# Moving four groups of on-chip buffers by 64 to 352 bytes in an attention and feed-forward kernel

## The chip, the cores and the metric

The kernel runs on one core of one Trainium2 chip. A core has a matrix engine (TensorE, PE in the profile, with its weight loads shown apart as PEld), a vector engine (VectorE, DVE), a scalar engine (ScalarE, ACT), GpSimd (POOL), a queue engine (SyncE, SP) and 16 DMA engines. On-chip memory (SBUF) has 128 partitions; a tile has the same byte address in each of its partitions. The accumulators lie in a second memory, PSUM. The metric is the device time of one execution in microseconds. Before the change two runs took 795.97 and 796.78 us, median 796.38 us.

## The reference, cut to what matters

Attention within chunks of 64 tokens, for 8 batches of 8 heads with 576 tokens and 64 columns a head, and then a feed-forward layer on the 4608 tokens, with 512 model columns, 2048 hidden columns and a leaky rectifier with one slope for each hidden column:

```python
scores = scale * np.matmul(q_c, k_c.transpose(0, 1, 2, 4, 3))
scores = scores - np.max(scores, axis=-1, keepdims=True)
attn = np.exp(scores)
attn = attn / (np.sum(attn, axis=-1, keepdims=True) + 1e-09)
out = np.matmul(attn, v_c)
...
h = x @ w_in
g = np.maximum(h, 0.0) + alpha * np.minimum(h, 0.0)
return (g @ w_out).astype(np.float32)
```

## The kernel before, in words

Every wide product is made of three matmuls on numbers split into a rounded high part and the rest (`hi` and `lo`, type float32r): high by high, high by low, low by high. A wide matmul has 128 rows, 128 columns of weights and 512 moving columns, and each is preceded by its own load of weights.

The tokens are nine blocks of 512. Blocks 0 to 2 (`PLAIN`) are done directly: `first_layer` (L394) multiplies a weight tile `wi` by the tokens `xh` and `xl` into the PSUM tile `ps_h`; the rectifier makes the tile `g` and its split `gh`, `gl`; `ffn_out` (L430) takes 128-column slices of `gh` and `gl` as weights and the tile `wo` as the moving operand. While this runs, the weights are fetched into tiles named `raw`, `more`, `wi` and `wo` and split by DVE and ACT, the remaining attention is done a part at a time (`attn_scores` L246, `attn_softmax`, `attn_blocks`, `attn_values` L361), and sums and differences of weight quarters are written to DRAM.

Blocks 3 to 8 are done in three pairs by a seven-product scheme on 2 by 2 blocks: `first_product` (its matmuls are in `product`, L695), then `second_product` (L836). Their weights come back from DRAM through a ring of four buffers of 512 KB: `stream` (L636, issued from POOL's queue) fills in turn two buffers `raw` of the pool `stage` and the buffers `wi15` and `wo15` of the pool `const`. One buffer serves 12 matmuls, and a buffer is refilled when the matmuls that read it are done. The moving operands of L695 lie in `const`; those of L836 are made in turn in `gh` and `gl` (or `g`) of the pool `gp`, and in `ta`, `tb`, `more` (once `ob`) of `stage`.

Order and place: a list of tokens (`START`) and then the program's own order, with priorities for some parts, set the order on each engine. SBUF tiles come from pools that are laid out one after another in the order in which they are opened (L96 to L102): `small`, `const` (weights), `load` (q, k, v and the transposed softmax), `soft`, `xp` (x), `gp` (pieces of g), `stage` (staging tiles). Every tile from `const` on has a size that is a multiple of 512 bytes a partition, and `const` begins at byte 5120, so all of them begin at a multiple of 512.

Two of the small products matter for the argument. `attn_scores` takes as weights and as moving operand the same 64 columns of two tiles; `attn_values` takes columns h*64 on of `v_sb` as weights, and as moving operand two runs of 32 columns of `pT` that begin at (4*par+hp)*128 bytes (h = 2*hp + par):

```python
lhsT=q_sb[rows, 2 * hp + c],  rhs=kb[rows, 2 * hp + c],                       # L246
lhsT=v_sb[rows, h * C:(h + 1) * C],  rhs=p[rows, :, par * NP + hp],           # L361
```

Of the kernel before, what the change touches and what calls it, by code (L numbers as in the profile page):

```python
# [11 lines left out]
F32 = mybir.dt.float32  # L12
# [48 lines left out]
def tile_local_attention_prelu_ffn(  # L61
# [13 lines left out]
    P = 128  # L75
# [19 lines left out]

    small = ctx.enter_context(tc.tile_pool(name="small", bufs=1))  # L96
    const = ctx.enter_context(tc.tile_pool(name="const", bufs=1))
    load = ctx.enter_context(tc.tile_pool(name="load", bufs=1))
    soft = ctx.enter_context(tc.tile_pool(name="soft", bufs=1))
    xp = ctx.enter_context(tc.tile_pool(name="xp", bufs=2))  # L100
    gp = ctx.enter_context(tc.tile_pool(name="gp", bufs=2))
    stage = ctx.enter_context(tc.tile_pool(name="stage", bufs=2))  # L102
    dram = ctx.enter_context(tc.tile_pool(name="dram", bufs=1, space=bass.MemoryType.DRAM))
    ps_a = ctx.enter_context(tc.tile_pool(name="ps_a", bufs=1, space=bass.MemoryType.PSUM))
# [956 lines left out]
```

## Time and profile before

| | before |
|---|---|
| two runs, us | 795.97, 796.78 |
| the profiled execution, us | 797.23 |
| its span, first to last instruction, us | 795.5 |
| granted TensorE clock over the span | 1.000 |
| PE busy | 783.7 us (99%) |
| DVE busy | 650.7 us (82%) |
| ACT busy | 449.8 us (57%) |
| POOL busy | 205.9 us (26%) |
| DMA | 192.40 MB, mean 242 GB/s |

The profiled execution lasted 1.7 us longer than its span; that is time before the first and after the last instruction. Matmuls are pipelined: one lasts some 390 ns in the records while the next begins some 227 ns after it, so PE's busy time alone does not tell whether it could go faster; the distance between the starts does.

### The profile page before, as it was taken

What the parts mean: (1) busy time and instruction counts of PE and PEld (TensorE: products, weight loads), DVE (VectorE), ACT (ScalarE), POOL (GpSimd) and SP (SyncE); (2) the same over time, 40 slices, a digit from 0 to 9 for tenths busy, and PEclk for the clock granted to TensorE, in tenths of its full rate; (3) what the DMA queues carried; (4) which work ended last, traced back from release to release, by engine and by line L of the source; (5) the groups of instructions that cost most, each with busy time, mean ns of one, the idle gap of its engine ahead of it and who ended that gap; (6) DMA issues with size and microseconds to landing.
All of it is one profiled execution on the core that took longest, in us unless ns stands there. A gap on an engine that the chain in (4) does not pass through costs nothing.

```text
span 795.5 us, 15528 instructions
## 1 busy us (share of the span) xinstructions
PE 783.7 (99%) x5562; PEld 641.8 (81%) x5562; DVE 650.7 (82%) x1147; ACT 449.8 (57%) x1223; POOL 205.9 (26%) x326
## 2 busy tenths in 40 slices
PE   7999999999999999999999999999999999999998
PEld 6788888888878888888887788888887888888886
DVE  6999989997979976887799987777899856677875
ACT  6975545656667565656665636664565524354552
POOL 0053323442424420111112341111222421112232
PEclk9999999999999999999999999999999999999999
DMA  9769495566869675888767799876567985565788
GB/s 349 316 220 357 176 310 195 205 225 184 266 199 263 231 272 179 281 262 278 265 211 243 212 285 322 271 227 197 187 217 231 264 293 185 188 208 186 243 227 243
DMA packets 73404, 192.40 MB, mean 242 GB/s; under 512 B 11488, under 2 KB 18928, under 8 KB 73200
## 3 DMA queue, kind: packets, MB, share of 16 engines
q0 software_dynamic: 38272, 127.43, 50.4%
q1 hardware_dynamic: 34768, 63.60, 23.7%
q8 instruction: 44, 0.72, 0.4%
q10 hardware_dynamic: 288, 0.39, 0.2%
q14 instruction: 32, 0.26, 0.1%
HBM read 135.27 MB, written 42.99 MB: 224 GB/s over the span
## 4 chain that ended last, share of the span: by engine, by line
PE 91%; DVE 5%; ACT 3%; DMA 0%; issue 0%; SPq 0%; DVEq 0%; ACTq 0%
PE ps_o L695 29%; PE ps_o L836 16%; PE ps_h L394 16%; PE ps_b L836 8%; PE ps_ob L430 8%; PE ps_oa L430 8%; PE ps_a L361 2%; DVE wi L755 2%; PE ps_a L246 2%; DVE gl L655 1%; ACT wo L289 1%; ACT wi L289 1%; PE ps_h L897 1%; DMA k_sb<-kT 0%; DVE tb L655 0%; DVE more L655 0%
## 5 line engine op out<-in xcount | busy, mean ns | idle before, releaser
L394 PE MATMUL ps_h<-xh,wi 128*128 128x512 f32 x384 | 104.5, 393 | 0.2 <-ACT xh L346 0.2
L695 PE MATMUL ps_o<-wi,raw 128*128 128x512 f32 x252 | 99.1, 393 | 0.1
L695 PE MATMUL ps_o<-wo,raw 128*128 128x512 f32 x252 | 98.1, 389 | 0.0
L394 PEld LDWEIGHTS ps_h<-xh,wi 128*128 128x128 f32 x384 | 71.1, 188 | 15.3 <-ACT xh L346 0.4
L263 ACT ACTIVATE pr<-ps_a,mx 128x64 f32<-128x64 f32 x224 | 67.5, 328 | 0.9
L430 PE MATMUL ps_ob<-wo,gh 128*128 128x512 f32 x192 | 59.3, 390 | 1.1 <-ACT g L461 1.1
L430 PE MATMUL ps_oa<-wo,gh 128*128 128x512 f32 x192 | 59.9, 393 | 0.0
L695 PEld LDWEIGHTS ps_o<-wi,raw 128*128 128x128 f32 x252 | 47.3, 188 | 10.4 <-ACT wi L461 0.2
L695 PEld LDWEIGHTS ps_o<-wo,raw 128*128 128x128 f32 x252 | 47.3, 188 | 9.6
L394 PE MATMUL ps_h<-xl,wi 128*128 128x512 f32 x192 | 52.0, 390 | 0.0
L654 ACT CAST gh<-wi 128x512 fp32r<-128x512 f32 x45 | 28.1, 624 | 40.4 <-PE ps_o L836 29.4
L695 PE MATMUL ps_o<-wi,wo 128*128 128x512 f32 x126 | 49.6, 393 | 0.0
L695 PE MATMUL ps_o<-wi,wi 128*128 128x512 f32 x126 | 49.5, 393 | 0.0
L263 ACT ACTIVATION_READ_ACCUMULATOR pr<-ps_a,mx 128x1 f32 x224 | 49.2, 220 | 0.0
L695 PE MATMUL ps_o<-wo,wi 128*128 128x512 f32 x126 | 49.1, 389 | 0.0
L695 PE MATMUL ps_o<-wo,wo 128*128 128x512 f32 x126 | 49.1, 389 | 0.0
L408 ACT CAST gh<-g 128x512 fp32r<-128x512 f32 x48 | 30.2, 630 | 32.1 <-DVE g L382 24.8
L636 POOL DMA_DIRECT2D raw<-wi_a x42 | 22.4, 532 | 97.7 <-PE ps_o L695 86.2
L717 DVE TENSOR_TENSOR gh<-ps_o,gh 128x512 f32<-128x512 f32 x24 | 16.6, 691 | 37.3 <-ACT gh L716 21.0
L379 ACT ACTIVATE wo<-gh 128x512 f32<-128x512 f32 x24 | 15.2, 632 | 53.1 <-DVE gh L725 53.1
L636 POOL DMA_DIRECT2D raw<-wo_a x42 | 22.4, 532 | 85.5 <-PE ps_o L836 45.2
L430 PEld LDWEIGHTS ps_ob<-wo,gh 128*128 128x128 f32 x192 | 36.0, 188 | 9.0 <-ACT g L461 1.5
(295 smaller groups left out, 2138.8 us busy)
## 6 DMA issues: line engine op xcount, KB each, us to landing
raw<-wi_a POOLq DMA_DIRECT2D x42, 512.0 KB, 4.9
raw<-wo_a POOLq DMA_DIRECT2D x42, 512.0 KB, 4.3
wi<-wi_a POOLq DMA_DIRECT2D x21, 512.0 KB, 4.1
wo<-wi_a POOLq DMA_DIRECT2D x21, 512.0 KB, 4.2
wi<-wo_a POOLq DMA_DIRECT2D x21, 512.0 KB, 4.1
wo<-wo_a POOLq DMA_DIRECT2D x21, 512.0 KB, 4.4
k_sb<-kT SPq DMA_DIRECT2D x28, 256.0 KB, 4.7
q_sb<-qT SPq DMA_DIRECT2D x28, 256.0 KB, 3.8
```

The lines of the kernel that those rows point to most:

```text
L246: pe(nc.tensor.matmul(ps[c * C:(c + 1) * C, par, (NP + hp) * C:(NP + hp + 1) * C], lhsT=q_sb[rows, 2 * hp + c], rhs=kb[rows, 2 * hp + c], ...
L263: last = nc.scalar.activation(pr[:, g], sc3[:, g // NP, g % NP], AF.Exp, bias=mx[:, g], scale=SCALE, accum_out=sm[:, g])
L289: last = nc.scalar.activation(pr[:, g], sc3[:, g % 2, g // 2], AF.Exp, bias=mx[:, g], scale=SCALE, accum_out=sm[:, g])
L361: pe(nc.tensor.matmul(ps[par * C:(par + 1) * C, c, hp * C:(hp + 1) * C], lhsT=v_sb[rows, h * C:(h + 1) * C], rhs=p[rows, :, par * NP + hp] ...
L394: pe(nc.tensor.matmul(hps, lhsT=wi[f][:, l, k * P:(k + 1) * P], rhs=xx[:, k], start=(i == 0 and k == 0), stop=(i == 2 and k == NK - 1),))
L408: nc.scalar.copy(gh, g)
L430: pe(nc.tensor.matmul(o, lhsT=a[:, ts], rhs=wo[f][:, l], start=(f == first and i == 0), stop=(f == last and i == 2),))
L636: streamed[0] = nc.gpsimd.dma_start(out=f32(t), in_=units[side][n])
L654: hi = nc.scalar.copy(t_hi, t)
L695: pe(nc.tensor.matmul(ps, lhsT=w[:, l, k * P:(k + 1) * P], rhs=xx[:, xl], start=first and at == 0, stop=at == n - 1, skip_group_check=not ...
L717: nc.vector.tensor_tensor(t, d, t, op=ALU.add)
L836: pe(nc.tensor.matmul(ps[m], lhsT=w[:, l, m * P:(m + 1) * P], rhs=xx, start=i != 6 and j == 0 and n == 0, stop=j == JF - 1 and n == 2, ski ...
```

## The change

Four pools of one buffer each are opened in front of `load`, `xp`, `gp` and `stage`, and one small tile is made in each that nothing reads or writes. They take 64, 64, 128 and 96 bytes a partition.

```diff
     const = ctx.enter_context(tc.tile_pool(name="const", bufs=1))
+    shift_load = ctx.enter_context(tc.tile_pool(name="shift_load", bufs=1))
+    shift_load.tile([P, 16], F32, name="shift_load")
     load = ctx.enter_context(tc.tile_pool(name="load", bufs=1))
     soft = ctx.enter_context(tc.tile_pool(name="soft", bufs=1))
+    shift_xp = ctx.enter_context(tc.tile_pool(name="shift_xp", bufs=1))
+    shift_xp.tile([P, 16], F32, name="shift_xp")
     xp = ctx.enter_context(tc.tile_pool(name="xp", bufs=2))
+    shift_gp = ctx.enter_context(tc.tile_pool(name="shift_gp", bufs=1))
+    shift_gp.tile([P, 32], F32, name="shift_gp")
     gp = ctx.enter_context(tc.tile_pool(name="gp", bufs=2))
+    shift_stage = ctx.enter_context(tc.tile_pool(name="shift_stage", bufs=1))
+    shift_stage.tile([P, 24], F32, name="shift_stage")
     stage = ctx.enter_context(tc.tile_pool(name="stage", bufs=2))
```

The first byte of some tiles in the two built programs, and what is left modulo 512:

```
pool (tile)         before            after
const (wi15, wo15)  9216, 5120    0   9216, 5120      0
load (q_sb)         136192        0   136256         64
soft (pr)           152576        0   152640         64
xp (xh)             154624        0   154752        128
gp (g)              187392        0   187648        256
stage (raw)         199680        0   200032        352
stage (ob, the end) 228352            228704
```

The two programs have the same instructions in the same order on each of PE, DVE, ACT, POOL and SP, with the same tiles and the same waits; only the line numbers behind L97 are 2 to 8 higher.

## Rows read from the trace of the kernel before

**Rows 1.** The page: the span, the busy time of the engines, and the shares of the chain of work that ended last.

```profile
span 795.5 us, 15528 instructions
PE 783.7 (99%) x5562; PEld 641.8 (81%) x5562; DVE 650.7 (82%) x1147; ACT 449.8 (57%) x1223; POOL 205.9 (26%) x326
...
PE 91%; DVE 5%; ACT 3%; DMA 0%; issue 0%; SPq 0%; DVEq 0%; ACTq 0%
```

**Rows 2.** The same chain in order of time, some of its pieces: start in us, length in us, what, how many instructions.

```profile
45.08 2.72 PE ps_h L394 x12
47.80 1.36 PE ps_oa L430 x6
...
639.31 76.16 PE ps_o L695 x336
...
726.35 32.64 PE ps_o L836 x144
```

**Rows 3.** PE's instructions in order of time around one visit of the attention, at 322 us: start, length from the first start to the last end, line, count.

```profile
322.00 0.39 PE L695 MATMUL ps_o<-wi,wo 128*128 128x512 f32 x1
322.22 0.39 PE L695 MATMUL ps_o<-wo,wo 128*128 128x512 f32 x1
322.54 0.69 PE L361 MATMUL ps_a<-pT,v_sb 64*64 64x64 f32 x32
323.06 0.65 PE L246 MATMUL ps_a<-k_sb,q_sb 64*64 64x64 f32 x32
```

**Rows 4.** All instructions of L361, and of L246, of the whole span: count, and minimum, median and maximum of one in ns.

```profile
L361 PEld LDWEIGHTS ps_a<-pT,v_sb x896: 128/135/136, 163.7 to 551.8; 64*64 64x64 f32 x180
L361 PE MATMUL ps_a<-pT,v_sb x896: 217/218/268, 163.7 to 551.8; 64*64 64x64 f32 x180
...
L246 PEld LDWEIGHTS ps_a<-k_sb,q_sb x896: 129/135/136, 140.2 to 531.0; 64*64 64x64 f32 x180
L246 PE MATMUL ps_a<-k_sb,q_sb x896: 217/218/268, 140.2 to 531.1; 64*64 64x64 f32 x180
```

**Rows 5.** Busy time of the engines in ten stretches (PE, PEld, DVE, ACT, POOL in us with the number of instructions; then the granted clock, the busy share of the 16 DMA engines, and GB/s).

```profile
20.00:100.00 80.00, 78.56 (x644) 64.45 (x644) 76.72 (x151) 55.49 (x135) 23.34 (x31) 1.00 0.71 268
100.00:200.00 100.00, 100.00 (x732) 81.79 (x731) 89.84 (x172) 58.85 (x181) 33.38 (x45) 1.00 0.67 224
200.00:300.00 100.00, 98.90 (x902) 80.38 (x901) 86.25 (x166) 62.81 (x214) 34.90 (x47) 1.00 0.78 245
315.00:398.00 83.00, 83.00 (x775) 67.71 (x774) 64.31 (x111) 51.44 (x186) 14.27 (x27) 1.00 0.85 275
420.00:475.00 55.00, 54.62 (x239) 44.14 (x238) 49.80 (x82) 29.81 (x52) 18.94 (x30) 1.00 0.85 246
480.00:560.00 80.00, 80.00 (x702) 65.09 (x701) 60.81 (x102) 46.60 (x152) 14.29 (x27) 1.00 0.76 248
562.00:636.00 74.00, 73.56 (x323) 59.95 (x322) 67.36 (x110) 40.98 (x72) 22.64 (x37) 1.00 0.77 227
640.00:715.00 75.00, 75.00 (x332) 62.12 (x332) 49.19 (x75) 30.29 (x52) 14.43 (x28) 1.00 0.63 211
716.00:758.00 42.00, 42.00 (x187) 34.80 (x186) 34.80 (x57) 19.22 (x34) 9.31 (x18) 1.00 0.67 214
759.00:791.00 32.00, 32.00 (x142) 26.34 (x142) 20.37 (x33) 13.95 (x24) 11.91 (x17) 1.00 0.91 242
```

**Rows 6.** The weight ring: three issues in a row on POOL, in order of time (start, length, line, tile, and in brackets what ended POOL's idle time).

```profile
664.09 0.53 POOL L636 DMA_DIRECT2D raw<-wi_a  x1 [1.89 <-PE ps_o L695]
666.81 0.53 POOL L636 DMA_DIRECT2D raw<-wi_a  x1 [2.19 <-PE ps_o L695]
669.53 0.53 POOL L636 DMA_DIRECT2D wi<-wi_a  x1 [2.19 <-PE ps_o L695]
```

**Rows 7.** All 168 loads of L636: the time from issue to landing.

```profile
DMA to landing us min/median/max: 3.4/4.4/7.5
```

**Rows 8.** The costliest groups of DVE, of the whole span: count, busy us, mean ns of one, and the idle time before them with what ended it.

```profile
L411 DVE TENSOR_TENSOR gl<-g,gh 128x512 fp32r<-128x512 f32 x48 | 32.9, 684 | 4.9 <-ACT gh L408 4.7
L755 DVE TENSOR_TENSOR wi<-wo,wi 128x512 f32<-128x512 f32 x48 | 32.6, 684 | 0.0
L735 DVE TENSOR_TENSOR gl<-ps_o,g 128x512 f32<-128x512 f32 x48 | 31.8, 683 | 1.2 <-PE ps_o L695 1.2
```

**Rows 9.** The last pieces of the chain of work that ended last.

```profile
789.91 1.83 PE ps_o L836 x8
791.74 0.02 issue
791.76 0.42 DVE xh L791
792.18 0.33 DVEq L1057
```

## The prediction

> **What bounds the kernel.** I read the page first: its span and its chain of work that ended last [rows 1]. PE is busy 99% of the span and holds 91% of the chain; DVE has 5%, ACT 3%, DMA none to the percent. Whatever moves the time has to move PE, or to make PE wait where it does not wait now.
>
> Then the same chain in order of time, for the pace of the wide matmuls [rows 2]. 12 of `first_layer` take 2.72 us, 6 of `ffn_out` 1.36, 336 of `first_product` 76.16, 144 of `second_product` 32.64: each time 226.7 ns a matmul. The reader is to see that this pace does not depend on the line, on the tiles, or on whether the weights lie in `raw` or in `wi15` (the 336 hold both). There are 48 steps of 12 matmuls in L394 and as many in L430, and three pairs of 8 x 7 x 6 in L695 and in L836: 576 + 576 + 1008 + 1008 = 3168, at 226.7 ns 718 us of the span of 795.5. The rest is the start, the small matmuls and some short waits.
>
> Third the stretches [rows 5]: from 100 us on PE stands still for 1.9 us of the 641 us that the nine rows cover, at a granted clock of 1.00, which is 2.4 GHz. DVE is nearly full at the start (76.72 of 80 us), the DMA engines are busiest where the ring is refilled beside other traffic (0.85, 0.85 and 0.91).
>
> **The change, part by part.** No instruction is added, removed or moved, and no wait. The four tiles are never touched. They cost 352 bytes a partition at the end of the memory. What changes is where the tiles of five pools begin: 0 modulo 512 for the weights as before, 64 for q, k, v and the softmax, 128 for x, 256 for pieces of g, 352 for staging. An effect can come only by an engine, or a DMA engine, that takes another time for the same instruction at another address. Four places, each bounded from both sides.
>
> *Weight load against moving operand in PE.* These two reads are the only ones that run in a fixed step with each other, once per matmul, and before the change each wide matmul has both at 0 modulo 512. At 2.4 GHz 512 columns at one a clock would be 213.3 ns; the pace is 226.7, 32 clocks more. If all of that came from the two reads meeting at one place, it could go wherever they begin apart. So the bounds are 0 and 13.3 ns for each such matmul, and a loss is as open as a gain, since no wide matmul of this trace has them apart. The nearest rows are the small matmuls: in L246 weights and moving operand always begin at the same place modulo 512; in L361 they begin, by the quoted slices, 0, 256, 128, 384, 256, 0, 384 and 128 bytes apart (`hp` and `par` in order). 32 of either take 0.69 and 0.65 us from the first start to the last end [rows 3], and one of either 218 ns, its weight load 135 ns, at the median [rows 4]. L361 is the one of the two that follows a wide matmul, which may be the 0.04 us. With distances that take in all four multiples of 128, the two lines go alike. So I take 0 of the 13.3 ns.
>
> *DVE and ACT.* An instruction on 512 columns of two SBUF tiles takes 684 ns (L411, L755), one on a PSUM tile and an SBUF tile 683 ns (L735) [rows 8]. With one of its two inputs in another memory the place of the other cannot meet it, and yet it is not faster; so equal places cost nothing that different ones could give back. That different ones cost something no row can show. DVE holds 5% of the chain, ACT 3%; where DVE is fullest (20 to 200 us, 166.6 us busy of 180 [rows 5]) it has 13.4 us to spare, so 5% on each of its instructions there, 8.3 us, would fit but for waits at the start, where it has 3.3 us to spare and would need 3.8. I take 0, and 1 us as the upper end for 1 or 2% on the instructions at the start.
>
> *DMA.* Loads into `raw`, `more`, `q_sb`, `k_sb`, `v_sb`, the moves from `t3` to `pT`, stores from staging and x now begin off a multiple of 512; the DRAM side stays. What hides it: a buffer of the ring is issued every 2.72 us (666.81 to 669.53) and needed three turns later, 8.16 us, while it lands after 4.4 us at the median, 7.5 at most [rows 6, 7]. So 9% more on the slowest load, or 85% more on the median one, passes unseen. The engines' shares [rows 5] allow 1/0.91, some 10%, in the fullest stretch and 18% in the next. At the end the last output leaves `xh`, but PE, DVE and the queue's end close the chain [rows 9]. Lower bound 0, upper bound in the rivals; I take 0, the value where neither the ring nor the shares are reached.
> A rule of the Trainium skill speaks against this change ("DMA: Bandwidth & Descriptors", section "How a descriptor splits into AXI transactions"): a transfer that does not begin at a multiple of 256 bytes first fetches the bytes below its start for nothing. No run here shows it so far. If it holds on the SBUF side for reading and writing, my estimate from it is 3 beats on 128 for a 4 KB row of `raw` (2.3%), and 4 on 64 for a 2 KB row of x (6%); by that the sum would be some 0.1 us higher, at the end of the last output, and the ring would still be in time.
>
> *The memory's end.* It moves to byte 228704; nothing else lies there. Cost 0.
>
> **Sum.** 795.5 us of span and 1.7 around it are the 797.23 us of the profiled execution. Plus 0, 0, 0 and 0 is 797.2; the profiled execution is 0.85 us above the median of the two runs, 796.38. I forecast that median: **796.4 us**. The measurement of this kernel can tell some 2% from no change, and this lies within it.
>
> **Rivals.**
>
> *Faster: the reads of PE do meet.* Then the wide matmuls whose two operands now begin apart drop to at best 213.3 ns. L394: weights at 0, x at 128, all 576. L430: slices of `gh` and `gl` at 256, `wo` at 0, all 576. L695: the moving operands lie in `const` at 0, so only those with weights in `raw` at 352, 504 of 1008. L836: with weights in `wi15` and `wo15` all 504; with weights in `raw` only those whose moving operand is in `gp`, about half, 252, since `ta`, `tb`, `more` are at 352 too. Together 2412; by 13.3 ns that is 32 us: **764 us**, if DVE and the ring keep up. For it: the pace is exactly 32 clocks above the columns, everywhere, and everything lies at 0. Against it: the small matmuls [rows 3, 4], and that a constant over such different pairs looks more like a fixed step of the load than like a meeting. Chance 0.04.
> The skill's page "TensorE: Matmul & The Clock Gate" (section "Wait — 56ns, not 53.3ns?") gives 215.7 ns for 512 columns back to back, without a weight load between; the trace disagrees for this kernel's matmuls, with 226.7. By the page's figure as the floor this rival would give an estimated 26 us in place of 32, some 770 us.
>
> *Slower: the transfers.* The mechanism is that a packet that begins off a 512-byte place takes half as long again, because its row is cut in more pieces. The place is the ring and what runs beside it. About two thirds of the bytes touch a shifted tile (half of the ring, all of q, k, v, `pT` and staging), so the demand on the DMA engines grows by a third: 0.85 to 1.13, 0.91 to 1.21, 0.78 to 1.04, 0.77 to 1.03, 0.76 to 1.01. It decides from 1 on, so from a packet that costs 26% more in the stretches at 0.85. Price, stretch by stretch [rows 5]: 13% of 83 + 55 us, 21% of 32, 4% of 100, 3% of 74, 1% of 80, together 32 us, before PE's waits at the ring: **829 us**. For it: the shares are high, and this kernel has no transfer off a 512-byte place to judge by. Against it: 26% of 4096 bytes is 1,065 bytes, and no tile is shifted by more than 352. Chance 0.03.
>
> *In between: engines lose a little at unequal places.* 1 to 2% on DVE and ACT, seen in the first 200 us only, at most 3 us: 797 to 799, within 2% and inside the range.
>
> That the change does not do what it says is no rival: the built program has the tiles at the new places.
>
> **Chances and range.** 0.93 for no change that can be told, 0.04 for the first rival, 0.03 for the second. The three executions before lie within 1.26 us (795.97 to 797.23); twice that to either side of 796.4 covers another chip and the small costs above: 794 to 799 us. The rivals lie far outside and hold 0.07 together, so the range needs not reach them.
>
> **What would show it.** Right: the chain still has 76.16 us for 336 matmuls of L695 (its line 8 higher) and 2.72 for 12 of L394; PE idle in those nine stretches still some 2 us; the ring's landing near 4.4 and below 8.2 us; DVE's groups at 684 ns. Wrong by the first rival: in L695 two paces side by side, some 213 ns with weights in `raw` and 226.7 with weights in `wi` and `wo`. Wrong by the second: DMA shares near 1.00 in the stretches that are at 0.85, PE waiting for loads of `raw` but not so much for those of `wi15`. Wrong by a slower DVE: groups whose two inputs lie in different pools above 684 ns, and those with one input in PSUM unchanged.

## The result and the profile after

The changed kernel takes 807.43 us (two runs, 806.93 and 807.93) against 796.38 before: a ratio of 1.0129, 95% interval 1.0111 to 1.0147. I had forecast no change, 794 to 799 us. The change is smaller than 2%, but clear of the noise, and outside my range.

The page of the changed kernel, the lines that answer to [rows 1]:

```profile
span 805.2 us, 15528 instructions
PE 794.6 (99%) x5562; PEld 641.9 (80%) x5562; DVE 653.1 (81%) x1147; ACT 452.5 (56%) x1223; POOL 205.8 (26%) x326
...
PE 92%; DVE 5%; ACT 2%; issue 0%; DVEq 0%; ACTq 0%
```

The span grew by 9.7 us and PE's busy time by 10.9, with the same instructions, at a granted clock of 0.999 (1.000 before). PE did not begin to wait; it works longer. The chain in order of time, the pieces that answer to [rows 2] (lines are 8 higher):

```profile
44.54 2.79 PE ps_h L402 x12
47.33 1.38 PE ps_oa L438 x6
48.71 1.36 PE ps_ob L438 x6
...
645.81 77.56 PE ps_o L703 x336
...
734.49 33.42 PE ps_o L844 x144
```

The pace of 226.7 ns a matmul is gone in three of the four lines: 232.5 ns in L402 (2.79 / 12), 230.8 in L703, 232.1 in L844. Only `ffn_out` (L438) stays near it, with 1.36 us for 6 once it has settled. Inside L703 the two paces stand side by side, here in PE's instructions in order of time (start, length, line, tiles):

```profile
649.63 0.40 PE L703 MATMUL ps_o<-wo,raw 128*128 128x512 f32 x1
...
651.03 0.39 PE L703 MATMUL ps_o<-wo,raw 128*128 128x512 f32 x1
...
652.64 0.39 PE L703 MATMUL ps_o<-wi,wi 128*128 128x512 f32 x1
...
653.55 0.39 PE L703 MATMUL ps_o<-wi,wi 128*128 128x512 f32 x1
```

With the weights in `raw`, at 352 modulo 512 against moving operands at 0, six matmuls take 1.40 us from 649.63 to 651.03, 233 ns each. Some matmuls after the weights have passed to the ring's buffer in `const`, at 0, four take 0.91 us, 227 ns; the first five there still took 228 to 236. My first rival was to leave just this trace, two paces in one line by the place of the weights; only, the pace at unequal places is the slower one, not the faster.

Added up from start to start in the two traces, L402 takes 2.9 us more, L703 3.9, L844 4.2. L438 takes 0.8 less, since a wait of 1.1 us for ACT before it does not occur in this execution, and the beginning is 0.6 us shorter. Together 9.6 of the 9.7 us.

Equal places in one matmul are not enough. In L844 the places of weights and moving operand change every 6 or 12 matmuls, and there a matmul with both operands in `stage`, at 352, is slow too if it comes behind others (start, length, line, tiles):

```profile
745.47 0.40 PE L844 MATMUL ps_o<-ta,raw 128*128 128x512 f32 x1
...
746.86 0.39 PE L844 MATMUL ps_o<-more,raw 128*128 128x512 f32 x1
```

Six take 1.39 us between these two starts, some 232 ns each. Of L844's 4.2 us, 1.5 fall on matmuls whose own operands begin 0 or 256 apart, and so do 0.5 of L703's 3.9.

What did not change: DVE's groups, here one whose two inputs now begin 352 bytes apart modulo 512, before and after (L411 of [rows 8], L419 here, keeps its 684 ns too, but both its inputs lie in `gp`), and the ring's landing (compare [rows 7]; POOL's loads, L644 here):

```profile
L655 DVE TENSOR_TENSOR tb<-wi,ta 128x512 fp32r<-128x512 f32 x24 | 16.4, 685 | 0.2
...
L663 DVE TENSOR_TENSOR tb<-wi,ta 128x512 fp32r<-128x512 f32 x24 | 16.5, 686 | 0.2
```

```profile
DMA to landing us min/median/max: 3.3/4.0/7.4
```

### The profile page after: what moved, and what is told of

Its sections match the earlier page's. It is cut to its first block, busy times and chain, and to the rows that moved or that the text cites. A ratio compares the mean times of both kernels' runs of the same rounds, so it can differ in the third digit from the quotient of the medians.

```text
span 805.2 us, 15528 instructions
## 1 busy us (share of the span) xinstructions
PE 794.6 (99%) x5562; PEld 641.9 (80%) x5562; DVE 653.1 (81%) x1147; ACT 452.5 (56%) x1223; POOL 205.8 (26%) x326
## 4 chain that ended last, share of the span: by engine, by line
PE 92%; DVE 5%; ACT 2%; issue 0%; DVEq 0%; ACTq 0%
PE ps_o L703 29%; PE ps_h L402 17%; PE ps_o L844 16%; PE ps_oa L438 8%; PE ps_b L844 8%; PE ps_ob L438 8%; PE ps_a L369 2%; DVE wi L763 2%; PE ps_a L254 2%; DVE gl L663 1%; ACT wo L297 1%; ACT wi L297 1%; PE ps_h L905 1%; DVE tb L663 0%; DVE more L663 0%; ACT xh L354 0%
## 5 line engine op out<-in xcount | busy, mean ns | idle before, releaser
L402 PE MATMUL ps_h<-xh,wi 128*128 128x512 f32 x384 | 106.2, 397 | 0.2 <-ACT xh L354 0.2
L703 PE MATMUL ps_o<-wi,raw 128*128 128x512 f32 x252 | 100.6, 399 | 0.1
L703 PE MATMUL ps_o<-wo,raw 128*128 128x512 f32 x252 | 99.8, 396 | 0.0
L402 PEld LDWEIGHTS ps_h<-xh,wi 128*128 128x128 f32 x384 | 71.1, 188 | 16.5 <-ACT xh L354 0.4
L438 PE MATMUL ps_oa<-wo,gh 128*128 128x512 f32 x192 | 60.2, 395 | 0.0
L438 PE MATMUL ps_ob<-wo,gh 128*128 128x512 f32 x192 | 59.3, 390 | 0.0
L703 PEld LDWEIGHTS ps_o<-wi,raw 128*128 128x128 f32 x252 | 47.4, 188 | 11.7 <-ACT wi L469 0.2
L703 PEld LDWEIGHTS ps_o<-wo,raw 128*128 128x128 f32 x252 | 47.4, 188 | 11.1
L402 PE MATMUL ps_h<-xl,wi 128*128 128x512 f32 x192 | 53.1, 395 | 0.0
L703 PE MATMUL ps_o<-wi,wi 128*128 128x512 f32 x126 | 49.7, 395 | 0.0
L703 PE MATMUL ps_o<-wi,wo 128*128 128x512 f32 x126 | 49.5, 393 | 0.0
L703 PE MATMUL ps_o<-wo,wi 128*128 128x512 f32 x126 | 49.3, 391 | 0.0
L703 PE MATMUL ps_o<-wo,wo 128*128 128x512 f32 x126 | 49.1, 390 | 0.0
L644 POOL DMA_DIRECT2D raw<-wi_a x42 | 22.3, 532 | 102.8 <-PE ps_o L703 89.1
L644 POOL DMA_DIRECT2D raw<-wo_a x42 | 22.4, 532 | 87.4 <-PE ps_o L844 46.2
L402 PEld LDWEIGHTS ps_h<-xl,wi 128*128 128x128 f32 x192 | 36.1, 188 | 8.7
```

What stands on the lines that cost most here:

```text
L402: pe(nc.tensor.matmul(hps, lhsT=wi[f][:, l, k * P:(k + 1) * P], rhs=xx[:, k], start=(i == 0 and k == 0), stop=(i == 2 and k == NK - 1),))
L438: pe(nc.tensor.matmul(o, lhsT=a[:, ts], rhs=wo[f][:, l], start=(f == first and i == 0), stop=(f == last and i == 2),))
L644: streamed[0] = nc.gpsimd.dma_start(out=f32(t), in_=units[side][n])
L703: pe(nc.tensor.matmul(ps, lhsT=w[:, l, k * P:(k + 1) * P], rhs=xx[:, xl], start=first and at == 0, stop=at == n - 1, skip_group_check=not ...
```

## The experiments

**Theories.** A: in PE the read of the moving operand and the load of weights disturb each other, by the distance of their places modulo 256 bytes. B: PE's reads are disturbed by the DMA engines, DVE or ACT, which now work on tiles off a multiple of 512. C: the place of a tile counts, not the distance between two.

**Chains of matmuls alone (`sweep`).** The kernel is replaced by 35 chains of 48 wide matmuls on two tiles that begin at the same place modulo 512, with nothing beside them (w and x below are bytes from there):

```diff
+    def mm(i, w, x):
+        return dict(lhsT=W[:, w // 4 + i % 4 * P:w // 4 + (i % 4 + 1) * P], rhs=X[:, x // 4 + i % 4 * 512:x // 4 + (i % 4 + 1) * 512],
+                    start=i == 0, stop=i == N - 1)
...
+    for i in range(N):
+        nc.tensor.matmul(ps, **mm(i, 0, 128))
```

> This kernel leaves out the whole computation: it loads two tiles, runs 35 chains of 48 wide matmuls (128 columns of weights, 512 moving columns, float32r) with nothing beside them, one chain for each place of the weights (w) and of the moving operand (x), in bytes modulo 512, and writes one result over the outputs. Theory A (in PE the read of the moving operand and the load of the next weights disturb each other, by the distance x - w modulo 256): 226.7 ns a matmul, so 10.9 us for 48, at x - w = 0 and 256, 230 to 236 ns (11.0 to 11.3 us) at the distances that the changed kernel showed (128, 160, 352, 416), also where both are moved by the same amount 10.9 us. Theory B (PE's reads are disturbed by the DMA or the other engines, which work on tiles off a multiple of 512): all chains 10.9 us, as nothing runs beside them. Theory C (the place of a tile itself, not the distance): the chains with w = x = 32 and w = x = 128 are slow too. Open: whether some distance gives less than 226.7 ns.

The chain of the profile has one piece for each chain of matmuls. The places (w, x) of the lines are, in order: L40 (0, 0), L42 (0, 4), L52 (0, 64), L60 (0, 128), L64 (0, 160), L74 (0, 240), L76 (0, 256), L82 (0, 352), L86 (0, 416), L98 (256, 0), L102 (128, 128), L104 (64, 192).

```profile
21.26 10.88 PE ps L40 x48
32.14 11.38 PE ps L42 x48
...
88.08 11.00 PE ps L52 x48
...
132.47 11.15 PE ps L60 x48
...
154.83 11.24 PE ps L64 x48
...
210.92 10.89 PE ps L74 x48
221.80 10.92 PE ps L76 x48
...
254.93 11.21 PE ps L82 x48
...
277.33 11.24 PE ps L86 x48
...
344.50 10.89 PE ps L98 x48
...
366.30 10.93 PE ps L102 x48
377.23 11.14 PE ps L104 x48
```

10.88 us is 226.7 ns a matmul; the slow chains have 229 (64 apart) to 237 ns (4 apart). The distances of the changed kernel, 128, 160, 352 and 416, give 232 to 234. Zero and 256 give 226.7 once settled, and so does moving both by 128 (its 10.93 us hold nine slower matmuls at the start). Nothing else runs, so theory B cannot make these differences, and (128, 128) speaks against C. No distance is faster than 0. The chain at 240 did not fit, and was tried again below.

**Only x moved (`x_only`).** x goes to 128 modulo 512, and the pools behind it return to 0:

```diff
+    shift_xp = ctx.enter_context(tc.tile_pool(name="shift_xp", bufs=1))
+    shift_xp.tile([P, 32], F32, name="shift_xp")
     xp = ctx.enter_context(tc.tile_pool(name="xp", bufs=2))
+    shift_gp = ctx.enter_context(tc.tile_pool(name="shift_gp", bufs=1))
+    shift_gp.tile([P, 96], F32, name="shift_gp")
     gp = ctx.enter_context(tc.tile_pool(name="gp", bufs=2))
```

> Only x is moved, to 128 modulo 512; g and staging are put back to a multiple of 512. Theory A: only the first layer's matmuls (weights at 0, x at 128) slow down, from 2.72 to 2.79 us for 12, together +3 us: 799.0 to 800.0 us, ratio 1.004; the other three lines keep 226.7 ns. Theory B: x is touched by few transfers before the three pairs, so no more than +1 us, 796 to 797.5 us.

800.18 us against 796.77 of the kernel before on the same chip, ratio 1.004, interval 1.0025 to 1.0055. The chain (the first layer is L398, the others L699 and L840):

```profile
72.72 2.79 PE ps_h L398 x12
...
641.92 76.16 PE ps_o L699 x336
...
728.96 32.64 PE ps_o L840 x144
```

Only the first layer is slower, and by what A says.

**Only staging moved (`stage_only`).** 352 bytes in front of `stage` alone:

```diff
+    shift_stage = ctx.enter_context(tc.tile_pool(name="shift_stage", bufs=1))
+    shift_stage.tile([P, 88], F32, name="shift_stage")
     stage = ctx.enter_context(tc.tile_pool(name="stage", bufs=2))
```

> Only the staging tiles are moved, to 352 modulo 512. Theory A: the first layer and ffn_out keep 226.7 ns; L695 with weights in raw (distance 160) goes to some 234 ns, L836 with weights in raw and gh or gl moving, or weights in wi15 or wo15 and more, ta or tb moving, to 232 to 235 ns; together +7 to +9 us: 803.5 to 805.5 us, ratio 1.010. Theory B: the ring's loads and the staging carry most of the shifted traffic, so most of the 11 us as well, but spread over all matmuls of the three pairs, also those of L695 with weights in wi15 and wo15.

805.20 us, ratio 1.011, interval 1.0092 to 1.0128.

```profile
72.30 2.72 PE ps_h L396 x12
...
643.55 77.56 PE ps_o L697 x336
...
732.23 33.42 PE ps_o L838 x144
```

The first layer is as before, and the two lines of the pairs are as slow as in the changed kernel, to the hundredth of a microsecond. Pieces of g lie at 0 here and at 256 there; it makes no difference. The two parts give 0.4 and 1.1%, and the whole 1.3%: they add up within their intervals.

**All moved alike (`all_together`).** The 352 bytes stand in front of the weights, so everything behind moves:

```diff
+    shift_const = ctx.enter_context(tc.tile_pool(name="shift_const", bufs=1))
+    shift_const.tile([P, 88], F32, name="shift_const")
     const = ctx.enter_context(tc.tile_pool(name="const", bufs=1))
```

> Weights, loads, x, g and staging are all moved by the same 352 bytes, so that every distance between them is 0 again, while every transfer begins off a multiple of 256 and 512. Theory A: 796.4 us, ratio 1.000 within 0.2%, and 226.7 ns in all four lines. Theory B and theory C: 805 us or more, since now all transfers and all tiles begin off a multiple of 512.

797.51 us against 796.77, ratio 1.0011, interval 0.9998 to 1.0023.

```profile
72.15 2.72 PE ps_h L396 x12
...
639.37 76.16 PE ps_o L697 x336
...
726.41 32.64 PE ps_o L838 x144
```

All paces are back, while the transfers, DVE and ACT work on tiles at 352 modulo 512 (all but the small tiles of the first pool). That ends theories B and C. What odd places cost the transfers is at most the interval's 0.2%.

**All moved by 256 (`all256`).** Does the distance count modulo 256 or 512 in the whole kernel?

```diff
+    shift_load = ctx.enter_context(tc.tile_pool(name="shift_load", bufs=1))
+    shift_load.tile([P, 64], F32, name="shift_load")
     load = ctx.enter_context(tc.tile_pool(name="load", bufs=1))
```

> One small tile of 256 bytes in front of the loads: loads, x, g and staging all begin at 256 modulo 512, the weights at 0. Theory A with modulo 256: all distances are 0 or 256, so 226.7 ns in all four lines and 796.4 us, ratio 1.000 within 0.2%. If the distance counts modulo 512: x against weights, g against wo, raw against the operands in const are all 256 apart, and the time is that of the changed kernel or more, 805 us and up.

797.08 us against 796.89, ratio 1.0004, interval 0.9993 to 1.0015.

```profile
638.26 76.16 PE ps_o L697 x336
...
725.30 32.64 PE ps_o L838 x144
```

All paces are those of the kernel before, so the distance counts modulo 256.

**The rest of the change (`load_g`).** Loads at 64 and pieces of g at 256, as in the change, staging at 256, x at 0:

```diff
+    shift_load.tile([P, 16], F32, name="shift_load")
...
+    shift_xp.tile([P, 112], F32, name="shift_xp")
...
+    shift_gp.tile([P, 64], F32, name="shift_gp")
```

> The rest of the change: loads and softmax at 64 as in the change, pieces of g at 256 as in the change, staging at 256 in place of 352, x and weights at 0. All distances between the two operands of wide matmuls are 0 or 256, the attention's small matmuls, DVE, ACT and the transfers work on tiles at 64. Theory A: 796.4 us, ratio 1.000 within 0.2%. If the loads' place costs something in the attention's small matmuls, its DVE work or the transfers, this shows it: 1 us or more.

796.84 us against 797.05, ratio 1.000, interval 0.9986 to 1.0014. The place of the loads costs nothing that can be told.

**More chains: finer places, other sizes, other types (`sweep2`).**

```diff
+        nc.tensor.matmul(**mm(i, 240))
...
+        nc.tensor.matmul(**mm(i, 0, cols=64))
...
+        nc.tensor.matmul(**mm(i, 128, n=256))
...
+        nc.tensor.matmul(**narrow(i, 64))
...
+        nc.tensor.matmul(**small(i, 128))
```

> Again the computation is left out: 27 chains of 48 matmuls with nothing beside them, float32r with the weights at 0 and the moving operand at x modulo 512. First chains: x = 12, 20, 228, 232, 236, 240, 244, 248, 252, 496, 128. If the earlier chain at 240 (226.7 ns) belongs to a band just below a multiple of 256, then 244, 248, 252 and 496 give 226.7 ns (10.9 us) too; if it was a single point they give 230 to 237 ns. Then 64 and 32 columns of weights, at x = 0 and 128: if the 13.3 ns above 213.3 at x = 0 are the load of 128 columns that does not fit beside the matmul, they shrink with the columns; if they are a fixed step of each matmul they stay. Whether the loss at 128 shrinks with fewer weight reads: theory A says yes. Then 256 and 128 moving columns at 0 and 128: theory A, a loss of the same 4 to 8 ns in each, or less as the overlap gets shorter. Then bfloat16 at 0, 64, 128: open. Last, 64 by 64 float32 matmuls as in the kernel's attention, at 0, 128 and 64: if they show no difference, the small matmuls on which my zero rested could not show the effect at all; if they show one, L361 should have shown it and theory A lacks something.

The lines below: L60 x = 20, L68 240, L74 252, L76 496; L80 and L84 64 and 32 columns of weights at x = 0; L88 and L90 256 moving columns at 0 and 128; L92 and L94 128 moving columns at 0 and 128. The pieces of L98 are the bfloat16 chain at 64.

```profile
44.01 11.52 PE ps L60 x48
...
89.16 11.33 PE ps L68 x48
...
123.35 11.04 PE ps L74 x48
134.39 11.35 PE ps L76 x48
...
156.93 11.04 PE ps L80 x48
...
179.07 11.11 PE ps L84 x48
...
201.25 5.75 PE ps L88 x48
207.00 5.70 PE ps L90 x48
212.70 5.31 PE ps L92 x48
218.01 5.36 PE ps L94 x48
...
233.74 0.65 PE ps L98 x3
...
244.10 1.08 PE ps L100 x5
```

First, there is no band below a multiple of 256: the chain at 240 now takes 236 ns. Second, fewer weight columns do not help: 64 columns (230 ns) and 32 (231 ns) are slower at distance 0 than 128 columns (226.7). The reading in my expectation that the 13.3 ns are the part of the load that does not fit falls. At 128 apart the narrower weights take 231 ns (11.10 and 11.07 us for 48 with 64 and 32 columns, L82 and L86), so what the distance costs shrinks to about 1 ns or none, as theory A said; but only because distance 0 got slower. Third, at 128 apart the loss shows with 512 moving columns alone: with 256 or 128 the chains at 128 are within 1% of those at 0. Fourth, bfloat16 has none: 10.36 us for 48 from 233.74 to 244.10, 215.8 ns (chains at 0 and 128 alike). Its weight load lasts 98 ns in the records against 188 in float32r, and its 512 columns are half the bytes; which of the differences spares it is not shown. And the small matmuls of float32, 64 by 64, which answer to [rows 3, 4], in the groups of instructions by line, L104 (128 apart) and L106 (64 apart; count, busy us, mean ns of one, idle time before):

```profile
L106 PE MATMUL two<-raw 64*64 64x64 f32 x96 | 1.9, 220 | 1.6 <-issue 1.6
L104 PE MATMUL two<-raw 64*64 64x64 f32 x96 | 1.7, 218 | 0.0
```

One takes 218 and 220 ns, as in the attention, and once running four of them take some 58 ns at 0, 128 and 64 alike, start to start. No difference by distance shows in them.

**Which two reads (`sweep3`).** Places that alternate from matmul to matmul:

```diff
+        nc.tensor.matmul(ps, **mm(i, (0, 128), (0, 128)))
...
+        nc.tensor.matmul(ps, **mm(i, (0, 128), (128, 0)))
```

> The computation is left out: 19 chains of 48 wide float32r matmuls with nothing beside them. Which two reads disturb each other: the moving operand of a matmul and the load of the NEXT weights (they begin together in the trace), or the moving operand and its OWN weights' load? In the third chain the places alternate 0 and 128 for both, so that each matmul has its own weights at distance 0 and the next ones at 128; in the fourth they are swapped, so that its own are at 128 and the next ones at 0. If the next load counts: third chain 232 to 233 ns a matmul (11.2 us for 48), fourth 226.7 (10.9 us). If its own: the other way round. The same with 64 in the ninth and tenth (229 ns against 226.7). Moving operand alternating 0 and 128 with the weights at 0: half of the matmuls off, between the two. Weights or moving operand alternating 0 and 256: 226.7. Last: 240 after a chain at 0 and after one at 224 (the two earlier chains at 240 gave 226.7 and 236): if the entry decides, the two differ; 192 matmuls in a row at 128: if they settle, the last chains come down to 226.7, otherwise 232 to 233 throughout.

L43 has its own weights at distance 0 and the next ones at 128, L45 the other way round, L53 a moving operand at 0 and 256 in turn; L61 and L65 are the two chains at 240, L75 the last 48 of 192 at 128:

```profile
31.50 10.97 PE ps L43 x48
42.47 11.04 PE ps L45 x48
...
86.61 10.88 PE ps L53 x48
...
130.69 11.20 PE ps L61 x48
...
153.09 11.20 PE ps L65 x48
...
208.78 11.22 PE ps L75 x48
```

Neither answer came out: both alternations lie between, 228.3 and 230.0 ns once settled, so neither pair of reads alone sets the pace. Which reads meet stays open. The four chains at 240 took 226.7, 236, 233 and 233 ns, so away from a multiple of 256 the distance alone does not fix the pace. What else does is not shown: my test by the chain in front gave no difference, and the chain at 240 behind one at 224 took 226.7 ns in `sweep` and 233 here. At 0 and 256, with 128 columns of weights, it always came back to 226.7, after nine matmuls at most; at 128 it did not settle in 192.

## Why the prediction was wrong

*The frame held.* PE bounds the kernel, no instruction moved, and the time changed by what PE's wide matmuls took. The four places that I listed were all that could change, and the right one stood first, with the count of matmuls whose operands begin apart.

*The step that failed: "I take 0 of the 13.3 ns".* It rested on the small matmuls as the nearest rows [rows 3, 4]. The chains alone show that 64 by 64 float32 matmuls go alike at 0, 64 and 128 apart, and that at 128 the loss shows in float32r with 512 moving columns, not with 256 or 128, and not in bfloat16. The row was near in kind, but blind to the question. It showed that distance does not matter for small matmuls, and I carried it over to a loop with another size, another type and another pace. In place of the 0, the three slower lines take 11.0 us more, as much as the change between the medians, 11.05 us.

*The sign.* I wrote that a loss was as open as a gain, and then gave the gain a rival, 32 us, and the loss none; my slower rival was in the transfers. Measured, the places lose: 5 to 6 ns a matmul in the first layer, 7 ns in L703 with weights in `raw`, 6 to 8 in L844 with operands apart. The bound should have been put on both sides, and the range with it: the 13.3 ns on 2412 matmuls are 32 us either way, and the measured loss of 11 us would have been inside.

*Which matmuls.* The list of the first rival was right for the first layer and for L695; elsewhere it went wrong because it counted modulo 512. `ffn_out` (576), 256 apart, keeps its pace, and so, once settled, do the matmuls of L836 with weights in `wi15` or `wo15` and `gh`, `gl` moving. Some 1578 matmuls are apart modulo 256, not 2412, and they hold 8.9 of the 11.0 us; the other 2.1 us fall on matmuls at 0 or 256 behind them, for which the list has no place.

*The first rival's argument.* From everything lying at 0 I argued that the 32 clocks above the columns could be the two reads meeting there. That was wrong: 0 is the best place found, and at 256 moving columns the pace at 0 is 5.75 us / 48 = 119.8 ns, again 13 above the columns at one a clock (106.7). The page "TensorE: Matmul & The Clock Gate" of the Trainium skill (section "Wait — 56ns, not 53.3ns?"), with 215.7 ns for 512 columns, agrees with the bfloat16 chain here, 215.8 ns, though that chain has a weight load before each matmul; for float32r the measurement decides, 226.7 at best.

*DVE, ACT.* Right: 686 ns with inputs 352 apart, 685 before, and `all_together` with the tiles at 352 costs nothing clear.

*DMA.* Right, and the rival fell: the ring lands after 4.0 us at the median, 7.4 at most, PE waits for no load of it. The rule of the Trainium skill that spoke against the change, on transfers off a multiple of 256 ("DMA: Bandwidth & Descriptors", section "How a descriptor splits into AXI transactions"), would by my estimate have given 0.1 us here; in `all_together` nothing above the interval's 0.2% is seen, which neither shows nor excludes so little.

*Range and chances.* 0.07 for all movement was too little, because the one term with two open sides was closed by a single proxy. The range came from the spread of the runs, not from that term. I also wrote that the measurement can tell some 2% from no change; its interval here, 1.0111 to 1.0147, tells 1.3% from none.

## What to carry to other kernels

Where float32r matmuls with 512 moving columns follow each other, let the weights and the moving operands of all of them begin at the same place modulo 256 bytes. Pools whose tiles are all multiples of 256 bytes a partition do that by themselves; here a small odd tile in front of a pool cost some 3% of each matmul whose operands it set apart, and slowed some matmuls behind those. In bfloat16 the chains at 64 and 128 lost nothing. Read such a loss from the distance between starts in the chain, not from PE's busy share, which was 99% in both kernels; and before a row is used as the nearest witness, ask whether it could have shown the effect at all.

## What the runs showed of the hardware that I had not expected

- The pace of float32r matmuls with 512 moving columns depends on the distance between the places of weights and moving operand: 226.7 ns a matmul at 0 or 256, up to 240 ns (20 bytes apart). That it is PE's two reads that disturb each other is the reading that fits, since nothing else ran; the reads themselves were not seen.
- The slowing settles in time at 0: after the weights passed from `raw` to `const`, intervals of 228 to 236 ns came down to 226.7 within half a dozen matmuls. A change of place thus costs a few more slow ones behind it.
- Narrower weights do not shorten a float32r matmul: 230 and 231 ns with 64 and 32 columns at distance 0.
- The best pace differs by type, with 128 columns of weights loaded before each matmul: 215.8 ns in bfloat16, 226.7 in float32r. The load lasts 98 ns in the one and 188 in the other.
